# Pooled sums on TensorE in the first blocks, later x2 loads, and weights in rows of 2 KB

## The chip, the cores and the metric

The kernel runs on one core of a Trainium2 chip. Its engines are TensorE (PE in the profile; PEld is its weight load), VectorE (DVE), ScalarE (ACT), GpSimd (POOL) and SyncE (SP, which here only issues transfers). Each engine works through its own instructions in order, and semaphores tie the engines together. Transfers are issued on SP's and on ScalarE's queue and run on the same 16 DMA engines. The metric is the device time of one execution in microseconds, lower is better.

## The reference, cut to what matters

Three layers in fp32: an attention that is the sum of a pooled part (queries, keys and values averaged over 4 neighbouring tokens, the result repeated 4 times) and a local part (a band of 7 keys), then two feed-forward layers on all 2304 tokens.

```python
batch, n_heads, seq, head_dim = 4, 8, 576, 64; factor = 4
q_d = q.reshape(B, H, Sd, factor, D).mean(axis=3)      # k_d, v_d likewise
out_up = np.repeat(sm_attn(q_d, k_d, v_d), factor, axis=2)
mask = np.abs(pos[:, None] - pos[None, :]) < factor
scores = np.where(mask, scale * q @ k^T, -1e9)         # then softmax, @ v
x = out_up + out_local                                 # 2304 x 512
x = ((x @ w_a) * (x @ w_b)) @ w_out                    # d_ff 1536
h = x @ w_in; out = (h * clip(h + 3, 0, 6) / 6) @ w_out2   # d_ff 2048
```

## The kernel before

Large products run as three passes of a reduced fp32 format (fp32r): each operand is split into a first and a second part. Weights arrive as 64-bit numbers and are decoded on ScalarE and VectorE (`decode`): a tile of 1 MB, 128 partitions by 1024 numbers, is loaded into `raw`, one of two buffers, and passes through one step on ScalarE (`m`, L237), six on VectorE (L243 to L261), one more on ScalarE (L265) and one more on VectorE (L268), after which it is `wh`.

**The opening.** Attention is worked per batch b and group g of two heads. `pooled(b, g)` loads queries and keys side by side (`qk`; for the first batch the tile is called qk0, shown as qk) and values ordered by token within a neighbourhood of four (`vd` into `v` or `vraw`). It sums four tokens on VectorE (`sums`, L383; `add_v`, L378 and L379), multiplies (`score`, dsc, L392), takes the softmax (`top` on VectorE, `exps` on ScalarE, `inverse` and `norm` on VectorE), transposes on TensorE (`turn`, dpt), copies (`turned`, deT, ScalarE) and multiplies by the values (`pv`, dpo, L439); `keep` copies the result to `od`. `local(u)` does the same for a unit of 116 tokens (112 for the last of a batch, five units a batch) with scores sc (L479, L485), transposes pt (L516) and values po (L528); `total` adds the pooled part to po on VectorE (xf, L536), and `x_first` (ScalarE) and `x_second` (VectorE, L546) split the sum into the two parts of x.

**The first stage** (`job(n, f)`) multiplies the x of block n (2 or 3 units) by weight tile f, twice 12 matmuls (pab, L578), and stores the product of the two results, `a`, to `h_d`. **The second stage** (`second(n, f)`) loads `h` for a span of 512 tokens (256 in the last) on ScalarE's queue (L619), splits it on ScalarE (L623) and VectorE (L627), and multiplies (acc, L635); results go as `x2f` to `x2_d` (shown as x_d, L659). At the same time the weights w2o are decoded and stored again (`w_d`). **The third stage** (`inner`, `group`; ph, L747) loads x2 as `x2r` (L695) and **the fourth** (`outer`; oacc, L870) ends the kernel.

**Order.** All steps are handed to a planner (`Plan`) with an engine, an assumed duration, a due time (`want`), what they come after and which buffers they take. The planner plays the steps through with these assumed durations and writes each engine's instructions in the order in which they would begin. So a changed duration or due time moves instructions of all engines, also where the code is not touched. On the chip only that order, the semaphores and the buffers count.

Of the kernel before, what the change touches and what calls it, by code (L numbers as in the profile page):

```python
# [9 lines left out]
F32 = mybir.dt.float32  # L10
# [128 lines left out]
def fused_kernel(ctx: ExitStack, tc: tile.TileContext, qk, vt, vd, wab, wo, w2i, w2o, mask, out):  # L139
# [83 lines left out]
    def decode(src, want, put, tag, after=(), ahead=4, slack=1.0, raw=None, queue=None):  # L223
# [129 lines left out]
    def pooled(b, g, want):  # L353
# [21 lines left out]
        def add_v():  # L375
            v_ = T["v_"]
            T["v"] = v_[:, :, 0] if b == 0 else slot(ap, [HD, 2, P], F32, "dv", "dv")
            nc.vector.tensor_tensor(v_[:, :, 0:2], v_[:, :, 0:2], v_[:, :, 2:4], op=ALU.add)  # L378
            nc.vector.tensor_tensor(T["v"], v_[:, :, 0], v_[:, :, 1], op=ALU.add)  # L379

        def sums():
            T["s"] = slot(ap, [P, 2, SD], F32, "dqk", "dqk")
            nc.vector.tensor_reduce(T["s"], qks[b, g][:, :, HALO:HALO + S].rearrange("p a (s r) -> p a s r", r=FACTOR),  # L383
                                    axis=AX.X, op=ALU.add)

        def score():
            s = T["s"]
            sc = T["sc"] = two_banks("dsc")
            for a in range(2):
                for h in range(2):  # L390
                    r = slice(64 * h, 64 * h + 64)
                    nc.tensor.matmul(sc[:HD, h, a * SD:(a + 1) * SD], s[r, 0, a * HD:(a + 1) * HD], s[r, 1],  # L392
                                     start=True, stop=True)
# [40 lines left out]
        def pv():  # L434
            po = T["po"] = one_bank("dpo")
            for c in range(2):
                for h in range(2):
                    r = slice(64 * h, 64 * h + 64)
                    nc.tensor.matmul(po[r, :SD], T["v"][:, c, r], T["eT", c][:, h], start=(c == 0), stop=(c == 1))  # L439
# [9 lines left out]
        av = DVE(dve(768) + 0.06, want - 3, add_v, [lv], take=[] if b == 0 else ["dv"], give=[] if b == 0 else ["vraw"])  # L449
        i = DVE(dve(2 * S), want, sums, [ld], take=["dqk"])  # L450
        S_["sums", b, g] = i
        i = PE(0.5, want, score, [i], take=["s2"], give=["dqk"])
        i = DVE(dve(4 * SD) + 0.16, want, top, [i])
        i = ACT(4 * 0.47, want, exps, [i], take=["de"], give=["s2"])
        i = DVE(0.32, want, inverse, [i])
        i = DVE(dve(4 * SD), want, norm, [i])
        t = [PE(0.3, want, turn(c), [i], take=["b", "turn"], give=["de"] if c else []) for c in range(2)]
        t = [ACT(act(2 * SD), want, turned(c), [t[c]], take=["deT"], give=["b", "turn"]) for c in range(2)]
        i = PE(0.6, want, pv, [*t, av], take=["b", "pv"], give=["deT", "deT", "wh" if b == 0 else "dv"])
        S_["od", b, g] = ACT(act(SD), want, keep, [i, S_.get(("od", b, 0))], take=[] if g else ["od"], give=["b", "pv"])  # L460

    def local(u, want):
# [33 lines left out]
        def exps():  # L496
            e = L["e"] = slot(ap, [P, HP, 2, KB], F32, "e", "e")
            z = L["z"] = ap.tile([P, HP, 2], F32, tag="z", bufs=2, name="z")
            for p in range(HP):
                for h in range(2):  # L500
                    nc.scalar.activation(e[:, p, h], L["s4"][:, p, h], AF.Exp, bias=L["mx"][:, p, h:h + 1],  # L501
                                         scale=SCALE, accum_out=z[:, p, h:h + 1])
# [19 lines left out]
        def pv():  # L522
            po_ = one_bank("po")
            L["po"] = po_[:, :HP * UT].rearrange("d (p t) -> d p t", p=HP)
            for p in range(HP):
                for i in range(2):
                    for h in range(2):
                        nc.tensor.matmul(L["po"][64 * h:64 * h + 64, p, i * QB:(i + 1) * QB], v_[:, h, i, p],  # L528
                                         L["eT"][:, p, i * KB:i * KB + QB], start=True, stop=True)

        def total():
            xf = L["xf"] = slot(ap, [P, HP, UT], F32, "xf", "xf")
            n = tokens // FACTOR
            c = j * UT // FACTOR
            up = ods[b][:, :, c:c + n].unsqueeze(3).to_broadcast([P, HP, n, FACTOR])
# [618 lines left out]
```

## Time and profile before

| | |
|---|---|
| median of 3 runs | 973.01 us (971.87 to 974.76) |
| the profiled execution's own time | 975.95 us |
| its span in the trace | 974.2 us |
| TensorE busy | 927.7 us (95%) |
| VectorE busy | 766.0 us (79%) |
| ScalarE busy | 457.3 us (47%) |
| mean granted TensorE clock | 0.985 |

The span runs from the first to the last instruction; the execution's own time also holds what lies around it. A busy TensorE is not TensorE at its peak: the number of matmuls in a stretch and the granted clock say how fast it went.

### The profile page before, as it was taken

The page shows a single profiled execution, that of the slowest core. Times are in us where ns is not written, and L with a number is a line of the kernel's source. Part 1 is how long each engine was busy: PE and PEld are TensorE (multiplying, and loading weights), DVE is VectorE, ACT ScalarE, POOL GpSimd, SP SyncE. Part 2 cuts the span into 40 slices and gives each one's busy share as a digit, 9 for nine tenths or more (in the row PEclk, how much of TensorE's full clock was granted, in tenths as well). Part 3 has the DMA queues.
Part 4 walks back from the last instruction along what each step waited for, and adds up shares of the span by engine and source line. Part 5 has one row for each costly group of instructions (what it writes and reads, how often), then busy time and mean ns, then how long its engine had stood idle before and what let it go on. Part 6 is the DMA issues. An engine that isn't in the chain of part 4 may idle for free.

```text
span 974.2 us, 18526 instructions
## 1 busy us (share of the span) xinstructions
PE 927.7 (95%) x7040; PEld 869.7 (89%) x7040; DVE 766.0 (79%) x1390; ACT 457.3 (47%) x1164; POOL 5.2 (1%) x44
## 2 busy tenths in 40 slices
PE   3779999999999999999999898999999999999998
PEld 2568899999989999997877688999999999999998
DVE  6888898954746959686887644899898999997983
ACT  3765633445455424224444333545454665554551
POOL 1000000000000000000000000000000000000000
PEclk9988999999999999999999899999999999999999
DMA  8442755323314433325678664334327891815401
GB/s 259 173 122 82 243 163 192 127 84 99 112 49 132 169 136 133 131 95 204 214 241 271 219 211 147 104 142 164 122 108 256 274 295 43 265 39 167 159 17 49
DMA packets 90089, 151.21 MB, mean 155 GB/s; under 512 B 8208, under 2 KB 71696, under 8 KB 85648
## 3 DMA queue, kind: packets, MB, share of 16 engines
q1 hardware_dynamic: 80384, 132.54, 41.4%
q10 hardware_dynamic: 9616, 17.49, 5.7%
q8 instruction: 55, 0.90, 0.4%
q14 instruction: 34, 0.28, 0.1%
HBM read 100.19 MB, written 49.81 MB: 154 GB/s over the span
## 4 chain that ended last, share of the span: by engine, by line
PE 80%; DVE 9%; DMA 7%; ACT 2%; issue 2%; ACTq 0%; SPq 0%; DVEq 0%
PE pab L578 32%; PE ph L747 16%; PE oacc L870 15%; PE acc L635 9%; DMA h<-h_d 4%; PE po L528 2%; DVE in L678 2%; DMA vz<-vt 1%; PE sc L485 1%; PE pt L516 1%; PE dpo L439 1%; DVE e L843 1%; DVE w2o L1078 1%; PE dpt L424 1%; DMA raw<-wab 1%
## 5 line engine op out<-in xcount | busy, mean ns | idle before, releaser
L578 PE MATMUL pab<-x,wh 128*128 128x344 f32 (+2 forms) x2016 | 325.6, 320 | 1.9 <-DVE wh L268 1.7
L578 PEld LDWEIGHTS pab<-x,wh 128*128 128x128 f32 x2016 | 311.8, 192 | 4.7 <-DVE wh L268 2.0
L870 PE MATMUL oacc<-w2o,in 128*128 128x256 f32 x1512 | 182.1, 283 | 1.4 <-DVE in L678 1.4
L870 PEld LDWEIGHTS oacc<-w2o,in 128*128 128x128 f32 x1512 | 181.3, 191 | 2.2 <-DVE in L678 2.0
L747 PE MATMUL ph<-in,w 128*128 128x384 f32 x1008 | 177.3, 337 | 2.5 <-ACT in L675 2.3
L747 PEld LDWEIGHTS ph<-in,w 128*128 128x128 f32 x1008 | 176.7, 189 | 3.0 <-ACT in L675 2.5
L635 PE MATMUL acc<-h,wo 128*128 128x512 f32 (+1 forms) x720 | 156.5, 377 | 9.4 <-ACT h L623 8.3
L635 PEld LDWEIGHTS acc<-h,wo 128*128 128x128 f32 x720 | 126.7, 191 | 39.2 <-ACT h L623 10.8
L763 DVE TENSOR_TENSOR part<-ph,part 128x384 f32<-128x384 f32 x168 | 85.7, 549 | 9.6 <-PE ph L747 8.8
L584 ACT ACTIVATE a<-pab 128x344 f32<-128x344 f32 (+2 forms) x84 | 37.3, 447 | 95.8 <-PE pab L578 67.5
L771 ACT ACTIVATE r<-part,three 128x384 f32<-128x384 f32 x96 | 56.5, 613 | 52.9 <-DVE part L763 50.1
L587 DVE TENSOR_TENSOR a<-a,pab 128x344 f32<-128x344 f32 (+2 forms) x84 | 41.4, 493 | 50.3 <-PE pab L578 45.2
L627 DVE TENSOR_TENSOR h<-h 128x512 fp32r<-128x512 f32 (+1 forms) x60 | 37.4, 634 | 51.6 <-ACT h L623 51.3
L675 ACT ACTIVATE in<-gr 128x384 fp32r<-128x384 f32 x96 | 47.5, 521 | 41.0 <-PE oacc L870 31.2
L237 ACT ACTIVATE m<-raw 128x1024 f32<-128x1024 f32 x34 | 39.3, 1157 | 57.0 <-DVE raw L255 21.2
L623 ACT ACTIVATE h<-h 128x512 fp32r<-128x512 f32 (+1 forms) x60 | 34.9, 588 | 64.5 <-DMA h<-h_d 51.6
L678 DVE TENSOR_TENSOR in<-gr,in 128x384 fp32r<-128x384 f32 x96 | 49.5, 551 | 6.7 <-ACT in L675 6.2
L675 ACT ACTIVATE in<-e 128x384 fp32r<-128x384 f32 x72 | 36.5, 527 | 33.9 <-PE oacc L870 20.2
L774 DVE SCALAR_TENSOR_TENSOR r<-r,part 128x384 f32<-128x384 f32 x96 | 50.4, 548 | 1.2 <-ACT r L771 1.1
L501 ACT ACTIVATE e<-sc,mx 128x64 f32<-128x64 f32 x160 | 47.6, 328 | 5.5 <-DVE mx L494 4.4
L255 DVE SCALAR_TENSOR_TENSOR raw<-raw,m 128x1024 f32<-128x1024 uint32 x34 | 41.7, 1227 | 1.2
L261 DVE TENSOR_TENSOR raw<-raw 128x1024 f32<-128x1024 f32 x34 | 41.5, 1221 | 0.5
(82 smaller groups left out, 885.7 us busy)
## 6 DMA issues: line engine op xcount, KB each, us to landing
g_d<-r SPq DMA_DIRECT2D x96, 192.0 KB
gr<-g_d SPq DMA_DIRECT2D x48, 384.0 KB
h<-h_d ACTq DMA_DIRECT2D x48, 256.0 KB
raw<-wab SPq DMA_DIRECT2D x10, 1024.0 KB
h_d<-a SPq DMA_DIRECT2D x48, 172.0 KB
raw<-w2i SPq DMA_DIRECT2D x8, 1024.0 KB
raw<-w2o SPq DMA_DIRECT2D x8, 1024.0 KB
qk<-qk SPq DMA_DIRECT2D x14, 576.0 KB
```

The lines of the kernel that those rows point to most:

```text
L255: nc.vector.scalar_tensor_tensor(out=lo.bitcast(F32), in0=lo, scalar=2.0 ** -52, in1=m, op0=ALU.mult, op1=ALU.mult)
L261: nc.vector.tensor_tensor(v, v, lo.bitcast(F32), op=ALU.add)
L501: nc.scalar.activation(e[:, p, h], L["s4"][:, p, h], AF.Exp, bias=L["mx"][:, p, h:h + 1], scale=SCALE, accum_out=z[:, p, h:h + 1])
L578: nc.tensor.matmul(T[k], wab_t[f][:, x, c], xs[n][:, g, y, :nb], start=(g == 0 and i == 0), stop=(g == KC - 1 and i == 2))
L635: nc.tensor.matmul(accs[n][e], wo_t[f // 2][:, x, c], hs[n, f][:, y], start=(f == 0 and i == 0), stop=(f == F1 - 1 and i == 2))
L675: nc.scalar.activation(x[0][:, 0], src(), AF.Copy)
L678: nc.vector.tensor_tensor(x[0][:, 1], src(), x[0][:, 0], op=ALU.subtract)
L747: nc.tensor.matmul(acc[k], t[:, x, g * P:(g + 1) * P], X[k, g][0][:, y], start=(g == 0 and n == 0), stop=(g == 1 and n == 2))
L763: nc.vector.tensor_tensor(s[name], acc[k], s[other], op=ALU.add)
L771: nc.scalar.activation(T["r"], src(), AF.Relu, bias=three)
L774: nc.vector.scalar_tensor_tensor(out=T["r"], in0=T["r"], scalar=6.0, in1=src(), op0=ALU.min, op1=ALU.mult)
L870: nc.tensor.matmul(acc[n][e], X[n, k][0][:, x, e * P:(e + 1) * P], t[:, y], start=(k == 0 and i == 0), stop=(k == K - 1 and i == 2))
```

## The change

It has five parts. (1) In the first batch (`soon`), VectorE sums only the keys; the scores take the queries of the four tokens apart, as four matmuls into one accumulation, and the value product takes the four values apart in the same way. (2) In the units of the first three blocks that have all 116 tokens (seven units), TensorE adds the pooled part: a matmul of the identity with `od`, each column repeated four times, opens the accumulation of po, and x is split from po itself. (3) The four x2 loads of the first pair in the third stage come after the step `second(last span, 1)`. (4) A weight tile lies in memory as four blocks of 128 rows of 2 KB, no longer as 128 rows of 8 KB. (5) The first two weight tiles are loaded on SP's queue, no longer on ScalarE's; `exps` of a unit is four steps instead of one, and some due times and assumed durations change.

```diff
         def load():
             T["raw"] = slot(xp if raw == "x" else dp, [P, W], mybir.dt.uint64, raw or "raw", "raw")
-            (queue or nc.sync).dma_start(T["raw"], src)
+            (queue or nc.sync).dma_start(T["raw"].rearrange("p (a c) -> p a c", a=CUT), src.rearrange("a p c -> p a c"))
...
-    def pooled(b, g, want):
+    def pooled(b, g, want, soon):
...
+            a = slice(1, 2) if soon else slice(0, 2)
             T["s"] = slot(ap, [P, 2, SD], F32, "dqk", "dqk")
-            nc.vector.tensor_reduce(T["s"], qks[b, g][:, :, HALO:HALO + S].rearrange("p a (s r) -> p a s r", r=FACTOR),
-                                    axis=AX.X, op=ALU.add)
+            nc.vector.tensor_reduce(T["s"][:, a], tokens()[:, a], axis=AX.X, op=ALU.add)
...
+                part = slice(a * HD, (a + 1) * HD)
+                for i in range(FACTOR if soon else 1):
+                    for h in range(2):
+                        r = slice(64 * h, 64 * h + 64)
+                        nc.tensor.matmul(sc[:HD, h, a * SD:(a + 1) * SD], tokens()[r, 0, part, i] if soon else s[r, 0, part],
+                                         s[r, 1], start=(i == 0), stop=(not soon or i == FACTOR - 1))
...
+            v = [T["v_"][:, :, i] for i in range(FACTOR)] if soon else [T["v"]]
             for c in range(2):
-                for h in range(2):
-                    r = slice(64 * h, 64 * h + 64)
-                    nc.tensor.matmul(po[r, :SD], T["v"][:, c, r], T["eT", c][:, h], start=(c == 0), stop=(c == 1))
+                for i, x in enumerate(v):
+                    for h in range(2):
+                        r = slice(64 * h, 64 * h + 64)
+                        nc.tensor.matmul(po[r, :SD], x[:, c, r], T["eT", c][:, h], start=(c == 0 and i == 0),
+                                         stop=(c == 1 and i == len(v) - 1))
...
-        av = DVE(dve(768) + 0.06, want - 3, add_v, [lv], take=[] if b == 0 else ["dv"], give=[] if b == 0 else ["vraw"])
+        av = lv if soon else DVE(dve(768) + 0.06, want - 1, add_v, [lv], take=["dv"], give=["vraw"])
...
+            if soon:
+                nc.tensor.matmul(L["po"].rearrange("p a (s r) -> p a s r", r=FACTOR), ident, pooled_part(), start=True, stop=False)
...
+            if soon:
+                L["xf"] = L["po"]
...
-        i = ACT(8 * 0.42, want, exps, [i], take=["e"], give=["s2"])
+        for p in range(HP):
+            i = ACT(2 * 0.31, want, exps(p), [i], take=[] if p else ["e"], give=["s2"] if p == HP - 1 else [])
...
-            return DMA(NB, want - 12 if p else want - 6, run, S_["x2d", m[t]] + ([] if p == 0 else [opened]),
+            return DMA(NB, want - 12 if p else want - 6, run,
+                       S_["x2d", m[t]] + [S_["second", len(spans) - 1, 1] if p == 0 else opened],
                        take=["x0" if p == 0 else "L"])
...
-        local(u, t)
+        local(u, t, m < 3 and unit_tokens(u) == UT)
...
-                                queue=nc.scalar if f < 2 else None)
+                                queue=None)
...
+        w = w.reshape(-1, P, CUT, w.shape[2] // CUT).transpose(0, 2, 1, 3)
         res[name] = np.ascontiguousarray(w).view(np.uint64)
```

What the planner makes of it is seen best at three places. A row's line is that of its own kernel, so line numbers differ between the two.

TensorE, the program's first rows, before: the four groups' scores stand together, then transposes, the values of the first group, and the first local scores.

```order
L392 MATMUL dsc<-dqk 72x144 x16
L424 MATMUL dpt<-ident,de 72x72 x8
L439 MATMUL dpo<-deT,v_146 64x144 x4
L424 MATMUL dpt<-ident,de 72x72 x4
L479 LDWEIGHTS ident_88
L479 MATMUL sc<-mask_sb,ident_88 128x256
```

The same place in the changed kernel:

```order
L398 MATMUL dsc<-dqk,qk_113 72x144 x16
L398 MATMUL dsc<-dqk,qk_117 72x144 x16
L398 MATMUL dsc<-dqk,qk_121 72x144 x16
L430 MATMUL dpt<-ident,de 72x72 x4
L490 LDWEIGHTS ident_88
L490 MATMUL sc<-mask_sb,ident_88 128x256
```

One group's scores are now 16 matmuls, and three groups stand ahead of the first transposes; the fourth group's scores come after the first local scores and the first group's values.

SP, the program's first rows, before (v are the values of the first batch, vz those of the local units, the qk row with x4 is the second batch):

```order
L365 DMA qk_113<-qk 128x2x576
L365 DMA qk_121<-qk 128x2x576
L370 DMA v_146<-vd 72x1024
L370 DMA v_156<-vd 72x1024
L370 DMA v_161<-vd 72x1024
L370 DMA v_178<-vd 72x1024
L473 DMA vz_105<-vt 64x512 x2
L473 DMA vz_106<-vt 64x512 x2
L365 DMA qk<-qk 128x2x576 x4
```

The same place in the changed kernel, from the last value load on:

```order
L370 DMA v_215<-vd 72x1024
L229 DMA raw<-wab 128x4x256 x2
L484 DMA vz_105<-vt 64x512 x2
L484 DMA vz_106<-vt 64x512 x2
L365 DMA qk<-qk 128x2x576 x4
```

The first two weight tiles, which before stood on ScalarE behind the exponentials and around the first two copies deT, now stand behind the values and ahead of the local values.

SP near the end of the second stage, before: three x2 loads behind a weight tile, with stores of decoded weights after them.

```order
L229 DMA raw<-w2o 128x1024
L695 DMA x2r<-x_d_5448 128x2x384 x2
L695 DMA x2r<-x_d_5446 128x2x384
L1040 DMA w_d_112<-ws 128x4x256
L1040 DMA w_d_112<-ws 128x3x256
```

In the changed kernel, further on: the four x2 loads stand after the stores of span 3 (the last with 512 tokens) and ahead of those of span 4.

```order
L683 DMA x_d_6245<-x2f 128x384
L683 DMA x_d_6247<-x2f 128x128
L719 DMA x2r<-x_d_5527 128x2x384
L719 DMA x2r<-x_d_5529 128x2x384 x2
L719 DMA x2r<-x_d_5527 128x2x384
```

The x2 loads have moved from behind a weight tile in the middle of the stage to its last span; the other transfers on SP there keep their order but for one pair of stores and for steps that pass each other.

## Rows read from the trace of the kernel before

**Rows 1.** The page: the span, and busy time of each engine.

```profile
span 974.2 us, 18526 instructions
...
PE 927.7 (95%) x7040; PEld 869.7 (89%) x7040; DVE 766.0 (79%) x1390; ACT 457.3 (47%) x1164; POOL 5.2 (1%) x44
```

**Rows 2.** Stretches: length, busy us (instructions) by engine, granted clock, DMA, GB/s.

```profile
0.00:55.00 55.00, 30.47 (x376) 21.68 (x376) 42.71 (x80) 29.52 (x126) 3.97 (x28) 0.97 0.69 213
55.00:115.00 60.00, 54.96 (x643) 48.95 (x640) 52.12 (x95) 37.58 (x160) 0.64 (x8) 0.89 0.40 126
441.60:607.50 165.90, 156.46 (x722) 126.55 (x720) 110.21 (x173) 65.00 (x113) 0.00 (x0) 0.98 0.67 218
```

**Rows 3.** Waits from 0 to 55 us: total, times, longest.

```profile
ACT m L237 <- DMA raw<-wab: 3.6, 1, 3.6
```

**Rows 4.** Timeline of TensorE in the opening: start, length, what, idle before.

```profile
6.73 1.24 PE L392 MATMUL dsc<-dqk 64*72 64x144 f32 x8 [6.73 <-DVE dqk L383]
...
19.80 1.23 PE L439 MATMUL dpo<-deT,v 72*64 72x144 f32 x8 [0.55 <-ACT deT L431]
...
43.51 1.96 PE L528 MATMUL po<-eT,vz 128*64 128x58 f32 x32 [0.69 <-ACT eT L520]
...
47.94 1.16 PE L528 MATMUL po<-eT,vz 128*64 128x58 f32 x32
...
55.01 2.91 PE L578 MATMUL pab<-x,wh 128*128 128x232 f32 x12
...
62.36 0.71 PE L392 MATMUL dsc<-dqk 64*72 64x144 f32 x8
```

**Rows 5.** Timeline of VectorE in the opening.

```profile
11.21 1.35 DVE L383 TENSOR_REDUCE dqk<-qk 128x288 f32<-128x1152 f32 x1 [2.18 <-DMA qk<-qk]
...
28.06 0.69 DVE L243 TENSOR_SCALAR m<-m 128x1024 f32<-128x1024 f32 x1 [2.55 <-ACT m L237]
...
53.74 0.59 DVE L546 TENSOR_TENSOR x<-xf,x 128x464 fp32r<-128x464 f32 x1
```

**Rows 6.** VectorE's groups from 0 to 55 us: count, busy us, mean ns.

```profile
L383 DVE TENSOR_REDUCE dqk<-qk 128x288 f32<-128x1152 f32 x5 | 6.8, 1352 | 6.9 <-DMA qk<-qk 6.6
...
L397 DVE TENSOR_REDUCE dmx<-dsc 72x4 f32<-72x576 f32 x4 | 3.0, 739 | 0.0
L345 DVE TENSOR_TENSOR e<-e,z 128x512 f32<-128x512 f32 x4 | 2.7, 682 | 0.0
L378 DVE TENSOR_TENSOR v<-v 72x512 f32<-72x512 f32 x4 | 2.7, 680 | 0.0
...
L379 DVE TENSOR_TENSOR v<-v 72x256 f32<-72x256 f32 x4 | 1.7, 421 | 0.1
...
L536 DVE TENSOR_TENSOR xf<-po,od 128x464 f32<-128x464 f32 x2 | 1.3, 636 | 0.3 <-PE po L528 0.3
```

**Rows 7.** Stretches again, columns as in rows 2.

```profile
20.00:25.00 5.00, 3.83 (x50) 2.57 (x48) 4.11 (x12) 2.07 (x11) 0.00 (x0) 1.00 1.06 410
535.00:550.00 15.00, 10.62 (x33) 7.62 (x32) 6.97 (x10) 3.22 (x5) 0.00 (x0) 0.77 0.71 242
560.00:575.00 15.00, 15.00 (x67) 12.31 (x66) 6.08 (x11) 3.90 (x7) 0.00 (x0) 1.00 0.88 288
595.00:600.00 5.00, 3.60 (x27) 3.06 (x26) 1.60 (x4) 1.57 (x4) 0.00 (x0) 1.00 0.80 263
```

**Rows 8.** The chain that ended last, near 534 us: start, length, what.

```profile
534.13 8.48 DMA h<-h_d
```

**Rows 9.** Timeline of TensorE from 530 to 548 us.

```profile
543.31 4.93 PE L635 MATMUL acc<-h,wo 128*128 128x512 f32 x10 [4.38 <-ACT h L623]
```

**Rows 10.** Timeline of SP's issues in the second stage.

```profile
533.67 0.78 SPq L229 DMA_DIRECT2D raw<-w2o  x1
534.50 3.00 SPq L695 DMA_DIRECT2D x2r<-x_d  x3
...
593.72 16.03 SPq L659 DMA_DIRECT2D x_d<-x2f  x8
```

More of the change, by code (lines that the diff above doesn't have):

```diff
@@ L448, in pooled, with local @@
         lv = DMA(290, early + 1 + 0.1 * g, load_v, take=["wh" if b == 0 else "vraw"])
-        av = DVE(dve(768) + 0.06, want - 3, add_v, [lv], take=[] if b == 0 else ["dv"], give=[] if b == 0 else ["vraw"])
-        i = DVE(dve(2 * S), want, sums, [ld], take=["dqk"])
+        av = lv if soon else DVE(dve(768) + 0.06, want - 1, add_v, [lv], take=["dv"], give=["vraw"])
+        i = DVE(dve(S if soon else 2 * S), want, sums, [ld], take=["dqk"])
         S_["sums", b, g] = i
-        i = PE(0.5, want, score, [i], take=["s2"], give=["dqk"])
+        i = PE(2.0 if soon else 0.5, want, score, [i], take=["s2"], give=["dqk"])
         i = DVE(dve(4 * SD) + 0.16, want, top, [i])
-        i = ACT(4 * 0.47, want, exps, [i], take=["de"], give=["s2"])
+        i = ACT(4 * 0.37, want, exps, [i], take=["de"], give=["s2"])
         i = DVE(0.32, want, inverse, [i])
         i = DVE(dve(4 * SD), want, norm, [i])
[L457 to L462, printed above, removed]
+        t = [PE(0.3, want, turn(c), [i], take=["b", "turn", "deT"], give=["de"] if c else []) for c in range(2)]
+        t = [ACT(act(2 * SD), want, turned(c), [t[c]], give=["b", "turn"]) for c in range(2)]
+        i = PE(1.6 if soon else 0.6, want, pv, [*t, av], take=["b", "pv"] + ([] if g else ["od"]),
+               give=["deT", "deT", "wh" if b == 0 else "vraw" if soon else "dv"])
+        S_["od", b, g] = ACT(act(SD), want, keep, [i, S_.get(("od", b, 0))], give=["b", "pv"])
+    def local(u, want, soon):
         L = {}
@@ L494, in top, with exps, run @@
             nc.vector.tensor_scalar(mx, mx, SCALE, None, op0=ALU.mult)
[L496 to L499, printed above, removed]
+        def exps(p):
+            def run():
+                if p == 0:
+                    L["e"] = slot(ap, [P, HP, 2, KB], F32, "e", "e")
+                    L["z"] = ap.tile([P, HP, 2], F32, tag="z", bufs=2, name="z")
                 for h in range(2):
-                    nc.scalar.activation(e[:, p, h], L["s4"][:, p, h], AF.Exp, bias=L["mx"][:, p, h:h + 1],
-                                         scale=SCALE, accum_out=z[:, p, h:h + 1])
+                    nc.scalar.activation(L["e"][:, p, h], L["s4"][:, p, h], AF.Exp, bias=L["mx"][:, p, h:h + 1],
+                                         scale=SCALE, accum_out=L["z"][:, p, h:h + 1])
+            return run
         def inverse():
@@ L548, in local @@
         n = HP * UT
-        ld = DMA(128, want - 25 if u < 2 else want - 5, load, [S_.get(("pv", u - 2))])
+        ld = DMA(128, want - 20 if u < 2 else want - 5, load, [S_.get(("pv", u - 2))])
         last = j == NU - 1
@@ L641, in second @@
         i = DVE(dve(nb), want - 12, h_second, [i])
-        i = PE(12 * (0.009 + 0.00044 * nb), want, products, [i, S_["wo", f // 2], S_["ps"]],
+        i = S_["second", n, f] = PE(12 * (0.009 + 0.00044 * nb), want, products, [i, S_["wo", f // 2], S_["ps"]],
                take=["q"] * KC if f == 0 else [],
@@ L940, in fused_kernel @@
             for g in range(HP):
-                pooled(u // NU, g, t - 0.05 + 0.01 * g)
-        local(u, t)
+                pooled(u // NU, g, t - 0.05 + 0.01 * g, u // NU < 1)
+        local(u, t, m < 3 and unit_tokens(u) == UT)
     for f in range(F1):
```

35 lines of the change are left out of this document (19 added, 16 removed).

## The prediction

> **What bounds the kernel now.** I read the page first, then stretches, then who waits for whom, then the rows of the stretches that lose time. TensorE is busy 927.7 of 974.2 us [rows 1], so only about 46 us can come from waits, and work added to TensorE where it never waits costs its full length. Three stretches hold nearly all of the loss [rows 2]. From 0 to 55 us TensorE is busy for 30.5 of 55 us. From 55 to 115 it is busy for 55.0 of 60, but at a granted clock of 0.89. From 441.6 to 607.5 (the second stage) it is busy for 156.5 of 165.9. VectorE is busy 42.7 of the first 55 us and 52.1 of the next 60, so in the opening it is nearly the bound. Of its waits one has to do with a transfer that the change moves: ScalarE stands 3.6 us before the first weight tile [rows 3].
>
> The opening ends where TensorE issues its first product of the first stage, at 55.01 [rows 4]. In front of it VectorE runs almost without a gap from 28.06, where it stops waiting for that weight tile, to 54.3, where the second unit's x is finished [rows 5].
>
> **What VectorE loses.** Half of each of four sums of queries and keys: 4 x 1.35 / 2 = 2.7 us; the value sums: 4 x (0.68 + 0.42) = 4.4 us; the addition of the pooled part in seven units: 7 x 0.63 = 4.4 us [rows 6]. Together 11.5 us, 8.4 of it before 55 us.
>
> **What TensorE gains.** A group's scores are 4 matmuls (8 rows of the profile, as each fp32 matmul shows two) and become 16; likewise its value products. Eight rows take 1.24 and 1.23 us early in the opening, but 0.71 at 62.36 [rows 4]. The clock column shows 1.00 for both, so for the early rows I go by their length, which is that of half speed. A group then pays 3.7 us more for scores and 3.7 for values at half speed, 2.1 and 2.1 at full. The pooled part by identity (128 x 464, fp32) has no row. Bounds from the score rows at full speed: 0.71 / 4 = 0.18 us for one of two matmuls of 144 columns that share the array, so 464 / 144 x 0.18 = 0.57 if a full-height one costs as much, 1.14 if it costs as much as the pair. I take 0.9, since nothing shares the array with it. So the opening's TensorE work grows by 17 us at full speed for the four groups and by 2.7 for three units.
>
> **Does TensorE reach full speed in time?** The product po took 1.96 us at 43.51 and 1.16 at 47.94, after 4.4 us almost without a pause [rows 4]. In the new order scores 0 and 1 stand behind each other as 64 rows, so I expect the change about 5 us after TensorE's start.
>
> **The new chain of the opening.** Score 0 starts at 6.73 - 0.7 = 6.0 (half a sum less) and takes 4 x 1.24 = 5.0 at half speed, to 11.0. Score 1 takes 2.7 (a little at half speed), to 13.7. Score 2 has its load by 11.2 [rows 5] and ends at 16.5. A transpose, a local score and a transpose take about 1.4, the values of group 0 take 2.8, and score 3, behind them, ends near 23.5. From there VectorE has all its work. What it does up to the second unit's x is what it did from 28.06 to 54.3 (26.3 us), without two additions of the pooled part (1.3) and one value sum (1.1, now later), with a full sum (1.35), the last group's maximum (0.74) and one rescaling (0.68) more [rows 6]: 26.7 us, which ends at 50.2. The weights no longer hold it: their two loads stand behind the values and not behind ScalarE's transposes, and should land near 20 instead of 26.9. The first product then begins near 51 instead of 55.0: **4 us**. TensorE has by then done one more po, one more transpose and one score (2.3 us at full speed) that it owed later; it still owes four identity products (3.6). VectorE is spared four more additions (2.5) in a stretch where it is 87% busy; I count 2. Opening: 4 + 2.3 - 3.6 + 2 = **4.7 us**. The order adds one wait: the first identity product stands on TensorE until ScalarE has copied the last group's pooled part, with the local scores of unit 4 and all else behind it; in the chain above that is at about 40, while VectorE has work until 50, so I count nothing (bound 1.5). The bank of po is held until the second part of x is done, one VectorE step (0.6) longer, of four banks: nothing. Scores read their weights at a step of four tokens, which no row shows: nothing, at worst the added 17 us twice, which is rival 1. The first local values now load behind the weights, near 22, and are needed near 40. Bounds of the opening: if the clock rises only after score 1, score 3 ends 2 to 5 us later and nothing is left; if all that VectorE loses came through, 11.
>
> **The second stage.** The worst place is 535 to 550: 33 matmuls where 560 to 575 has 67 [rows 7], at 0.224 us each, so 7.5 us lost, part idle and part at the lower clock (0.77). The chain shows a load of h of 8.48 us from 534.13, and TensorE's row at 543.31 that it had stood for 4.38 us [rows 8, 9]. Just ahead SP issued a weight tile of 1 MB (533.67) and, from 534.50, three of the four x2 loads of the third stage, 1.18 MB [rows 10]. The change takes these three away. At the 242 and 288 GB/s of these two windows they are 4.9 or 4.1 us of DMA time. So h that comes 4.1 us sooner leaves 0.3 of the 4.38, too short, I think, for the clock to fall. I count **6.5 us**.
>
> The x2 loads now stand on SP behind the first four of the eight stores at 593.72 [rows 10], so near 595.5. They are 1.57 MB: 6.0 us at 263 GB/s, over near 602, and the stage ends at 607.5, so the third stage does not wait for them. But they fall beside the last loads of h: 595 to 600 already has 27 matmuls of 128x256 where 44 fit at half of 0.224 us [rows 7]. I take 1.5 us of loss (bounds 0 and 3).
>
> Rows of 2 KB for the weights: a window in which weight tiles moved in 8 KB rows (20 to 25 us) shows 410 GB/s at a share of 1.06, one with shorter rows (595 to 600) 263 at 0.80, that is 387 against 329 at a full share [rows 7]. A tile of 1.05 MB then takes 3.2 us instead of 2.7, 0.5 longer. In the opening this is hidden by the 7 us that the weights are early; in the first stage by VectorE, which has a tile ahead; in the second, ScalarE stands in order before a weight tile, with h behind it, so up to 8 x 0.5 = 4 us could show. Against that h, on ScalarE's queue, meets shorter rows on SP's. Bounds: 4 us lost, 4 gained (the other short waits of this stage); I take 0.5 gained. SP needs more time to issue 512 rows than 128, but stands in no chain.
>
> The Trainium skill, DMA: Bandwidth & Descriptors (Specifications), states that 512 B is enough for line rate; by it the 0.5 us per tile would not exist and the loss bound of 4 us would be nothing. The two windows speak against it, but they differ in more than the rows; no run here shows weights in 2 KB rows.
>
> **Sum.** 4.7 + 6.5 - 1.5 + 0.5 = 10.2 us. The profiled execution took 975.95 us (span 974.2), which gives 965.8; it stands 2.9 above the median of the three runs (973.01), so I forecast 963.
>
> **Rivals.**
> 1. Slower: TensorE stays at half speed through the opening and becomes its bound. Added work: 4 x 7.4 + 3 x 1.8 = 35 us; with the 30.5 there now, from 6.0 on, the first product starts at 71.5, 16.5 later. Less 5.5 from the second stage: 984. It decides once the added work exceeds the 18.5 us in which TensorE is idle between 6 and 55 and what full speed takes off the old work. For it: every row up to 43 us is at half-speed length. Against it: 64 rows without a gap. Chance 0.11.
> 2. Only the second stage gains: TensorE's additions eat what VectorE gives: 967.5. Chance 0.18.
> 3. Only the opening gains: h is late for other reasons (ScalarE's order, weights that land later): 968.3. Chance 0.14.
> 4. The change does nothing that can be measured, as VectorE's savings turn into waits for TensorE and the x2 loads cost at 595 what they cost at 535: 973. Chance 0.10.
> 5. More: the shorter rows also let h pass the weights in the other short waits. The second stage is idle for 165.9 - 156.5 = 9.4 us [rows 2], 4.4 of it in the wait at 543; of the other 5.0 I give 3 to this: 960. For it: the load of h at 534 landed only when what was queued ahead of it on the other queue had passed. Against it: some of these waits end with ScalarE's order and not with a load. Chance 0.14. The Trainium skill, DMA: Bandwidth & Descriptors (Queues, rings and completion order), states that a DMA engine takes turns between its queues packet by packet; by it this case is the outcome, and no run here shows it.
> 6. The forecast, both gains: 963, itself from 957 to 967. Chance 0.33.
>
> **How the numbers follow.** A measurement of this kernel tells 0.3% (2.9 us) from no change. Cases 5, 6, 2 and 3 lie below 970, case 4 within 2.9 of 973, case 1 above; a few hundredths of 2 and 3 fall short of 970: faster 0.75, same 0.13, slower 0.12. The range leaves out case 1, the upper part of case 4, and gains beyond 18 us: 955 to 973.
>
> **What would show it.** Right: the first product near 51 us; the eight rows of scores as 32 rows, the later groups in about 2.8 us; no wait of ScalarE for the first weight tile; VectorE without a gap from about 23; 535 to 550 at full count and clock; the x2 loads at about 595, landing before 607. Wrong: early scores of 5 us each through 25 us; waits for DMA of h that move to 595 to 602; longer waits of ScalarE for weights in the second stage.

## The result and the profile after

The changed kernel takes 963.55 us (median of 4, 962.18 to 964.19); the kernel before took 972.44 beside it (970.22 to 974.76). The ratio is 0.9892, 95% interval 0.9866 to 0.9917, so it is faster by 0.8 to 1.3%. The forecast of 963 holds. Its terms don't, so the number is luck: the opening gave more than twice what was counted, and the second stage gave nothing.

The profiled execution took 964.17 us. Its page, as in [rows 1]:

```profile
span 962.2 us, 18896 instructions
...
PE 932.5 (97%) x7246; PEld 875.6 (91%) x7246; DVE 755.3 (78%) x1375; ACT 455.8 (47%) x1164; POOL 5.6 (1%) x44
```

TensorE does 206 more instructions and VectorE is busy 10.7 us less. Where the span's 12.0 us went is read from the first row of each stage on TensorE's timeline:

| first row of | before | after | gained in the stretch up to it |
|---|---|---|---|
| pab, the first product of the first stage | 55.01 | 51.12 | 3.9 |
| acc, the second stage | 441.62 | 430.21 | 7.5 |
| ph, the third stage | 609.87 | 599.52 | -1.1 |
| end of the span | 974.2 | 962.2 | 1.7 |

So 11.4 us were there before the second stage began. Three stretches of the changed kernel, columns as in [rows 2]:

```profile
0.00:51.00 51.00, 40.89 (x584) 33.15 (x584) 37.37 (x71) 31.14 (x134) 3.96 (x28) 0.90 0.80 234
51.00:111.00 60.00, 59.61 (x730) 52.26 (x725) 56.71 (x101) 37.95 (x141) 1.03 (x8) 1.00 0.43 131
430.20:599.50 169.30, 156.55 (x722) 127.40 (x720) 110.34 (x173) 65.59 (x116) 0.00 (x0) 0.98 0.68 216
```

The 60 us after the first product are the surprise: before, TensorE waited 5.0 us of them and its granted clock was 0.89; now it waits 0.4 at 1.00. At 0.89, 55 busy us hold 48.9 us of full-speed work, so about 6.0 us went to the clock. VectorE is busy 56.7 of the 60 us, where it was 52.1. The second stage is about as long as it was.

(For the opening the clock column reads too high; see the last section.) TensorE's timeline in the opening, to be held against [rows 4]:

```profile
6.07 9.25 PE L398 MATMUL dsc<-dqk,qk 64*72 64x144 f32 x96 [6.07 <-DVE dqk L388]
...
16.97 2.18 PE L448 MATMUL dpo<-deT,v 72*64 72x144 f32 x32
19.08 2.42 PE L398 MATMUL dsc<-dqk,qk 64*72 64x144 f32 x32
...
39.79 1.92 PE L539 MATMUL po<-od,ident 128*128 128x464 f32 x2 [0.39 <-ACT od L454]
...
45.14 1.30 PE L539 MATMUL po<-od,ident 128*128 128x464 f32 x2
...
49.17 0.94 PE L539 MATMUL po<-od,ident 128*128 128x464 f32 x2
...
51.12 2.94 PE L602 MATMUL pab<-x,wh 128*128 128x232 f32 x24
```

And VectorE's, against [rows 5]: decoding begins at 24.25 without a wait, and the second unit's x is finished at 49.0.

```profile
24.25 0.69 DVE L243 TENSOR_SCALAR m<-m 128x1024 f32<-128x1024 f32 x1
...
48.40 0.63 DVE L567 TENSOR_TENSOR x<-po,x 128x464 fp32r<-128x464 f32 x1
```

In the second stage the wait of [rows 9] has become two. TensorE's timeline, and below it the chain that ended last at the same places:

```profile
534.72 0.50 PE L659 MATMUL acc<-h,wo 128*128 128x512 f32 x1 [2.66 <-ACT h L647]
...
591.06 6.40 PE L659 MATMUL acc<-h,wo 128*128 128x256 f32 x36 [2.54 <-ACT h L647]
```

```profile
527.95 6.06 DMA h<-h_d
...
584.40 6.18 DMA h<-h_d
```

SP's issues, as in [rows 10], show what moves beside these two loads: the weight tile is still there in front of the first, and the x2 loads now stand in front of the second.

```profile
527.11 0.54 SPq L229 DMA_DIRECT2D raw<-w2o  x1
...
582.13 2.38 SPq L719 DMA_DIRECT2D x2r<-x_d  x4
```

### The profile page after: what moved, and what is told of

The parts are those of the page before. It is cut to its first block, busy times and chain, and to the rows that moved or that the text cites. A ratio compares the mean times of both kernels' runs of the same rounds, so it can differ in the third digit from the quotient of the medians.

```text
span 962.2 us, 18896 instructions
## 1 busy us (share of the span) xinstructions
PE 932.5 (97%) x7246; PEld 875.6 (91%) x7246; DVE 755.3 (78%) x1375; ACT 455.8 (47%) x1164; POOL 5.6 (1%) x44
## 4 chain that ended last, share of the span: by engine, by line
PE 84%; DVE 8%; DMA 6%; issue 1%; ACT 1%; ACTq 0%; SPq 0%; DVEq 0%
PE pab L602 32%; PE ph L772 18%; PE oacc L895 15%; PE acc L659 10%; DMA h<-h_d 4%; PE po L543 2%; PE dsc L398 2%; DVE in L702 2%; PE sc L496 1%; PE pt L529 1%; PE dpo L448 1%; DMA raw<-w2o 1%; DVE e L868 1%; PE po L539 1%; PE dpt L430 1%
## 5 line engine op out<-in xcount | busy, mean ns | idle before, releaser
L602 PE MATMUL pab<-x,wh 128*128 128x344 f32 (+2 forms) x2016 | 319.8, 317 | 0.1
L602 PEld LDWEIGHTS pab<-x,wh 128*128 128x128 f32 x2016 | 306.4, 188 | 3.6 <-issue 1.8
L659 PE MATMUL acc<-h,wo 128*128 128x512 f32 (+1 forms) x720 | 156.5, 378 | 10.7 <-ACT h L647 9.6
L651 DVE TENSOR_TENSOR h<-h 128x512 fp32r<-128x512 f32 (+1 forms) x60 | 37.5, 636 | 49.1 <-ACT h L647 48.9
L248 DVE SCALAR_TENSOR_TENSOR raw<-raw,m 128x1024 uint32<-128x1024 uint32 x34 | 41.5, 1221 | 0.2
```

Source lines behind the costliest of these rows:

```text
L248: nc.vector.scalar_tensor_tensor(out=hi, in0=hi, scalar=0xC0000000, in1=T["m"].bitcast(U32), op0=ALU.bitwise_and, op1=ALU.bitwise_or)
L602: nc.tensor.matmul(T[k], wab_t[f][:, x, c], xs[n][:, g, y, :nb], start=(g == 0 and i == 0), stop=(g == KC - 1 and i == 2))
L659: nc.tensor.matmul(accs[n][e], wo_t[f // 2][:, x, c], hs[n, f][:, y], start=(f == 0 and i == 0), stop=(f == F1 - 1 and i == 2))
```

## The experiments

The theory after this reading: the gain comes from the opening alone, and there from VectorE. Rivals: the second stage's edits are worth what was predicted and something else hides it; TensorE's fuller work holds the clock up; the earlier weights did it. Ratios are to the kernel before, timed beside it, and medians are over several executions; what is read from a trace is one execution. A change of code or of buffers also lets the planner order the steps anew; where that matters it is said.

### The second stage's two edits

**x2 loads released as before** (`x2_as_before`):

```diff
-                       S_["x2d", m[t]] + [S_["second", len(spans) - 1, 1] if p == 0 else opened],
+                       S_["x2d", m[t]] + ([] if p == 0 else [opened]),
```

> The changed kernel with the four x2 loads of the third stage released as before (no wait for the last span's second step). Theory (the opening gives nearly all, the move of the x2 loads trades the stall at 534 us for one at 591 us): within 1.5 us of the changed kernel, 962 to 965; the wait of acc for h near 591 us (2.5 us in the changed kernel) is gone, and one near 525 to 535 us grows to about 4.4 us. Rival (the move saves what the prediction counted, 6.5 less 1.5): 968 to 969.

961.22 us (957.04 to 968.06), ratio 0.9885 (0.9851 to 0.9919): no loss, against the rival. The six times lie up to 11 us apart, and the profiled execution is the fastest. In it the waits of acc for ScalarE's part of h in the second stage sum to 3.8 us, the longest 1.1, though three x2 loads (522.55) stand again right behind the weight tile, so the wait of 4.4 us that the theory expected did not come:

```profile
PE acc L659 <- ACT h L647: 3.8, 5, 1.1
```

**Weights in rows of 8 KB** (`rows_8k`):

```diff
-            (queue or nc.sync).dma_start(T["raw"].rearrange("p (a c) -> p a c", a=CUT), src.rearrange("a p c -> p a c"))
+            (queue or nc.sync).dma_start(T["raw"], src)
...
-        w = w.reshape(-1, P, CUT, w.shape[2] // CUT).transpose(0, 2, 1, 3)
```

> The changed kernel with a weight tile as 128 rows of 8 KB again. Theory (the rows' length is worth next to nothing): within 1.5 us of the changed kernel, 962 to 965. Rival A (short rows let h pass the weights): 966 to 968, with longer waits of acc for h in the second stage. Rival B (short rows cost, as the changed kernel's second stage is 1 us longer in the trace): 960 to 962.

963.43 us (961.82 to 965.99), ratio 0.9891 (0.9866 to 0.9916), which is that of the changed kernel. The second stage has much the same waits in both: here one of 1.94 us at 532 and one of 2.94 at 589.

**Both undone** (`opening_only`: the two diffs above together).

> The changed kernel with both undone: x2 loads released as before, weights in rows of 8 KB. What is left is TensorE's additions, the queue of the first two weights and the steps of the exponentials. Theory: 961 to 965, with the second stage starting near 430 us and lasting 168 to 169 us. Rival (the second stage's edits are worth the 5.5 us of the prediction): 968 to 970.

962.52 us (962.22 to 964.49), ratio 0.9884 (0.9861 to 0.9907). The second stage begins at 430.89 and lasts 167.3 us. Everything is there without the two edits. With the x2 loads back beside the long load of h, the wait there is 2.80 us, where the changed kernel has 2.66 without them:

```profile
531.65 0.50 PE L659 MATMUL acc<-h,wo 128*128 128x512 f32 x1 [2.80 <-ACT h L647]
```

**These two alone, on the kernel before** (`second_stage_only`).

> The kernel before with two of the edits alone: x2 loads after the last span's second step, weights in rows of 2 KB. Theory: no difference from before that can be measured, 970.5 to 974, second stage starting near 441 us. Rival (the prediction's sum for the second stage, 5.5 us): 966 to 968.

977.43 us, ratio 1.0028 (1.0009 to 1.0046): if anything slower. TensorE's timeline shows why the move brings nothing: the wait of 4.38 us [rows 9] is 3.09 without the x2 loads beside it, and two waits stand near where these now are (SP issues them at 593.09), where the kernel before has one of 1.32.

```profile
542.96 0.50 PE L635 MATMUL acc<-h,wo 128*128 128x512 f32 x1 [3.09 <-ACT h L623]
...
593.11 6.33 PE L635 MATMUL acc<-h,wo 128*128 128x256 f32 x48 [2.07 <-ACT h L623]
...
601.10 6.37 PE L635 MATMUL acc<-h,wo 128*128 128x256 f32 x36 [1.67 <-ACT h L623]
```

The kernel before, at its end of the stage:

```profile
598.35 9.18 PE L635 MATMUL acc<-h,wo 128*128 128x256 f32 x72 [1.32 <-ACT h L623]
```

There 72 matmuls take 9.18 us; here the last 36 take 6.37, at a granted clock of 0.76 from 600 to 607 us (1.00 there in the kernel before). The same count made for all six kernels, over the 720 matmuls of acc, shows what the move of the x2 loads is worth in each of its two places (us between the starts of two matmuls, one execution each):

| x2 loads and rows | from the 361st to the 421st | from the 661st to the last |
|---|---|---|
| early, 8 KB: before | 21.6 | 7.0 |
| late, 2 KB: `second_stage_only` | 19.2 | 10.8 |
| early, 8 KB: `opening_only` | 19.8 | 7.0 |
| late, 8 KB: `rows_8k` | 17.0 | 12.1 |
| early, 2 KB: `x2_as_before` | 15.9 | 7.0 |
| late, 2 KB: changed kernel | 17.3 | 11.7 |

In all three pairs the late loads cost 3.8 to 5.1 us at the end of the stage; in the middle they give 2.4 and 2.8 us in two pairs and lose 1.4 in the third, whose early side is the fastest execution of its kernel.

In the opening this kernel differs from the one before in the length of the rows alone, and there it is not free. Issued on ScalarE's queue at the same time (18.81 and 18.95), the first weight tile holds ScalarE up for 7.7 us, where it was 3.6 [rows 3], and the first product comes at 58.37, where it was 55.01:

```profile
ACT m L237 <- DMA raw<-wab: 7.7, 1, 7.7
```

### The opening: VectorE's relief or TensorE's work

**VectorE sums again** (`vector_sums`): all else as changed.

```diff
-                pooled(u // NU, g, t - 0.05 + 0.01 * g, u // NU < 1)
-        local(u, t, m < 3 and unit_tokens(u) == UT)
+                pooled(u // NU, g, t - 0.05 + 0.01 * g, False)
+        local(u, t, False)
```

The due time and buffers of `add_v` for the first batch are those of before.

> The changed kernel with all of TensorE's additions undone: VectorE sums queries and values and adds the pooled part, as before; queue of the first weights, steps of the exponentials, x2 loads and 2 KB rows as in the changed kernel. Theory A (the gain comes from VectorE's 11.5 us alone) and theory B (it comes from TensorE being kept at work, so that its clock does not fall in the 60 us after the first product): both 971 to 976, first product near 55 us, granted clock of the next 60 us about 0.9. Rival (the earlier weights and the finer steps give it): 963 to 966.

974.93 us, ratio 1.0015 (0.9992 to 1.0039): the whole gain is gone. The weights were early here too (VectorE's decoding begins at 24.59), and the first product comes at 52.19, not near 55 as expected. But in the 60 us after it TensorE waits 4.5 us at a granted clock of 0.91 (the profiled execution, 982.02 us, is the slowest of the ten):

```profile
52.20:112.00 59.80, 55.31 (x648) 49.63 (x646) 55.13 (x102) 37.96 (x157) 0.64 (x8) 0.91 0.47 148
```

**The same with TensorE's work added to no use** (`vector_sums_and_pe_work`): each pooled score four times, pooled values four times over, the identity product ahead of po, all overwritten.

```diff
-                for i in range(FACTOR if soon else 1):
+                for i in range(FACTOR if b == 0 else 1):
...
+            for c in [0] * (6 if b == 0 else 0):
+                for h in range(2):
+                    r = slice(64 * h, 64 * h + 64)
+                    nc.tensor.matmul(po[r, :SD], T["v"][:, c, r], T["eT", c][:, h], start=True, stop=True)
```

> The kernel of the run above with TensorE's work of the changed kernel added to it without use: each pooled score four times over, the pooled values four times over, the identity product ahead of po, all overwritten by the result as before. VectorE is relieved of nothing. Theory A (VectorE's relief): no gain, 973 to 980. Theory B (the clock): granted clock at 0.97 or more in the 60 us after the first product, and 965 to 970, though TensorE has 15 to 20 us more to do.

987.62 us, ratio 1.016 (1.0122 to 1.0197). The work costs 12.7 us and does not hold the clock: 0.87 and 0.81 in 60 to 80 and 80 to 100 us. Theory B falls.

```profile
60.00:80.00 20.00, 18.24 (x202) 15.82 (x201) 17.08 (x35) 9.58 (x41) 0.00 (x0) 0.87 0.37 114
80.00:100.00 20.00, 17.12 (x218) 12.75 (x218) 17.25 (x32) 13.86 (x66) 0.00 (x0) 0.81 0.10 34
```

**VectorE relieved, TensorE not loaded** (`no_pe_work`): one query and one value of four are used and the pooled part is left out in seven units, so its output lacks these.

```diff
-                for i in range(FACTOR if soon else 1):
+                for i in range(1):
...
-            v = [T["v_"][:, :, i] for i in range(FACTOR)] if soon else [T["v"]]
+            v = [T["v_"][:, :, 0]] if soon else [T["v"]]
...
-            if soon:
-                nc.tensor.matmul(L["po"].rearrange("p a (s r) -> p a s r", r=FACTOR), ident, pooled_part(), start=True, stop=False)
```

> The changed kernel without what TensorE takes over: the pooled scores of the first batch use one query of four, its pooled values one value of four, and the seven units leave out the pooled part (so the output lacks these). VectorE is relieved as in the changed kernel. Theory A: at least as fast as the changed kernel, 955 to 963. Theory B: the first product comes earlier, but the clock falls again in the 60 us behind it (0.95 or less), 964 to 970.

960.23 us, ratio 0.9884 (0.9851 to 0.9916). Theory A holds. Behind the first product TensorE has its full clock here too (columns as in [rows 2]), so theory B's loss does not come:

```profile
0.00:49.50 49.50, 33.93 (x387) 24.34 (x387) 37.84 (x72) 31.35 (x138) 3.96 (x28) 1.00 0.84 245
49.50:110.00 60.50, 58.36 (x723) 52.75 (x722) 56.99 (x101) 37.38 (x138) 0.95 (x8) 1.00 0.43 133
```

Its second stage begins at 428.27, 1.9 us before the changed kernel's: that is what TensorE's 206 rows cost in the end. Most of them go into time in which TensorE waited: in the opening it stands still for 15.6 us here and for 10.1 in the changed kernel.

**The pooled part on VectorE again** (`vector_pooled_part`): `local(u, t, False)`, the sums stay on TensorE.

> The changed kernel with the pooled part added by VectorE again in the seven units (no identity product); queries and values still summed on TensorE. Theory A: VectorE has 4.4 of its 11.5 us again, 966 to 969. Theory B: TensorE loses 7 us of its 24 us of added work, most of it at full clock behind the first product, 963 to 966.

968.86 us, ratio 0.9958 (0.9934 to 0.9982), 5 us above the changed kernel for seven additions of 0.63 us on VectorE, 4.4 in all. Theory A's number. The trace shows where they count: the first product comes 2.7 us earlier (48.47), with no identity product on TensorE ahead of it, but from there to acc it takes 383.9 us instead of 379.1.

### The opening: the queue of the first weights

**The first two weights on ScalarE's queue again** (`weights_on_act`); the orders of TensorE and VectorE are those of the changed kernel.

```diff
-                                queue=None)
+                                queue=nc.scalar if f < 2 else None)
```

> The changed kernel with the first two weight tiles loaded on ScalarE's queue again. Theory A (VectorE is the bound of the opening, so each wait of VectorE there counts): ScalarE again stands some 3 us before the first tile, VectorE's decoding begins near 27 us instead of 24.3, and the time is 965 to 967. Rival (the tile is early enough on either queue, VectorE has other work): 962 to 965.

974.43 us, ratio 1.0011 (0.9987 to 1.0036). Both theories missed it: this edit alone also loses the whole gain (the profiled execution, 971.23 us, is the second fastest of the ten). ScalarE's timeline shows two waits, and VectorE's and TensorE's what they do (three views, one after the other):

```profile
20.12 0.41 ACT L437 ACTIVATE deT<-dpt 72x288 f32<-72x288 f32 x1 [3.77 <-DMA vz<-vt]
...
31.14 1.12 ACT L237 ACTIVATE m<-raw 128x1024 f32<-128x1024 f32 x1 [4.30 <-DMA raw<-wab]
```

```profile
32.29 0.69 DVE L243 TENSOR_SCALAR m<-m 128x1024 f32<-128x1024 f32 x1 [3.50 <-ACT m L237]
```

```profile
59.52 2.95 PE L602 MATMUL pab<-x,wh 128*128 128x232 f32 x24
```

The copy deT at 20.12 needs no transfer. It stands behind the issue of the weight tile (19.68), which by the trace waits until a load of local values on the other queue has landed (why for that load, no run here shows); so ScalarE stands for 3.8 us with a group's softmax behind it, and for 4.3 more until the tile is there. The first product comes at 59.52 and acc at 438.63, both 8.4 us later than in the changed kernel. The Trainium skill, DMA: Bandwidth & Descriptors (Issuing engines are not separate DMA queues), states that transfers run on the same 16 DMA engines whoever starts them, and that another issuing engine only saves the time to initiate. Here the queue was worth 8.4 us, by when the tile is issued (19.68 here, 5.25 on SP's queue) and by what stands behind the issue on its engine. Part of it belongs to the rows of 2 KB: with them the tile lands 11.4 us after its issue here, while in the kernel before ScalarE goes on with it 8.0 us after its issue (18.95 to 26.91).

The four kernels with rows of 2 KB and late x2 loads side by side (ratios to before):

| | weights on ScalarE's queue | on SP's queue |
|---|---|---|
| VectorE adds | 1.0028 | 1.0015 |
| TensorE adds | 1.0011 | 0.9892 |

Neither edit alone gives anything clear of the intervals; together they give 1.4%. Where each one counts is read from the traces (us, one execution each):

| | first product | from there to acc |
|---|---|---|
| before | 55.01 | 386.6 |
| `second_stage_only`: VectorE adds, ScalarE's queue | 58.37 | 382.0 |
| `vector_sums`: VectorE adds, SP's queue | 52.19 | 390.6 |
| `weights_on_act`: TensorE adds, ScalarE's queue | 59.52 | 379.1 |
| changed kernel: TensorE adds, SP's queue | 51.12 | 379.1 |

The queue decides when the first product comes, the additions how long the stretch behind it takes. While VectorE still adds, a first product that comes 6.2 us earlier is paid back behind it (8.6 us, in an execution that is the slowest of its kernel); with VectorE relieved, the stretch behind is as short with either queue, and the late tile costs its 8.4 us in the opening alone.

The upper left kernel of the square also lacks the steps of the exponentials and the other due times and durations, and the change moves more than its list says: TensorE's steps, no longer ScalarE's, take the buffers deT, eT and od. What these are worth by themselves was not run.

### What holds the second stage

**Five buffers for h** (`h_five_buffers`), paid for with two of three buffers for the copies of acc:

```diff
-            "hg1": 1, "xo": 3, "q": 8, "ws": 2, "x0": 4, "L": 24, "c": 14}
+            "hg1": 2, "xo": 1, "q": 8, "ws": 2, "x0": 4, "L": 24, "c": 14}
...
-        return slot(pools["p3" if f % 4 == 3 else "p2"], [P, 2, NC], F32R, f"hg{f % 4 // 3}", name)
+        return slot(pools["p3" if f % 5 >= 3 else "p2"], [P, 2, NC], F32R, f"hg{int(f % 5 >= 3)}", name)
```

> The changed kernel with five buffers for h instead of four, paid for by one buffer for the copies of acc instead of three. A step of the second stage is 12 matmuls of 0.224 us, 2.7 us, so four buffers hide a load, its split and its wait for a turn only up to about 8 us. Theory C (the waits near 534 and 591 us are loads of h that take longer than four buffers hide, whatever is beside them): the waits of acc for h fall from 9.6 us to under 5, 958 to 961. Rival D (the transfers as such are the limit there, or the single copy buffer gives the waits back): 963 to 968.

958.53 us (955.75 to 960.53), ratio 0.984 (0.9798 to 0.9882): faster than the kernel before, and its slowest execution lies below the changed kernel's fastest, though the two intervals touch. TensorE's waits in the second stage (us in total, times, longest), first those of the changed kernel:

```profile
PE acc L659 <- ACT h L647: 9.6, 6, 2.7
PE ph L772 <- ACT in L699: 2.1, 1, 2.1
```

And with five buffers:

```profile
PE ph L772 <- ACT in L699: 6.5, 1, 6.5
PE acc L659 <- ACT h L647: 0.7, 1, 0.7
```

The 9.6 us in six waits of the changed kernel are 0.7, and the stage lasts 159.3 us instead of 169.3. About 4.5 us of it go back at its end, where ph waits 6.5 us instead of 2.1: with one buffer left, each copy of acc waits for the store before it, as ScalarE's timeline shows.

```profile
584.29 0.38 ACT L676 ACTIVATE x2f<-acc 128x256 f32<-128x256 f32 x1 [1.81 <-DMA x_d<-x2f]
586.49 0.38 ACT L676 ACTIVATE x2f<-acc 128x256 f32<-128x256 f32 x1 [1.82 <-DMA x_d<-x2f]
```

**The same with the x2 loads as before** (`h_five_buffers_x2_as_before`).

> The same five buffers, with the x2 loads released as before. Theory C: the three x2 loads in the middle of the stage are hidden too, 956 to 960. Rival D: 961 to 967.

957.94 us (956.33 to 959.24), ratio 0.9835 (0.9795 to 0.9875): the same. Acc waits 1.8 us for ScalarE's part of h, so the three loads in the middle are hidden. The planner orders the steps anew with the buffers; that is not separated from the fifth buffer itself.

**The loads of h on GpSimd's queue** (`h_on_pool_queue`):

```diff
-            nc.scalar.dma_start(h[:, 1].bitcast(F32), h_d[f][:, lo:hi])
+            nc.gpsimd.dma_start(h[:, 1].bitcast(F32), h_d[f][:, lo:hi])
```

> The changed kernel with the loads of h on GpSimd's queue, so that they stand behind no work of ScalarE. Theory E (the wait near 534 us comes from h loads that ScalarE issues late, as it stands in order before a weight tile): the wait there goes to about 1 us, the waits of acc for h halve, 958 to 961. Rival (h is late because of what moves beside it or for want of buffers): 962 to 966, waits as in the changed kernel.

966.25 us (963.26 to 967.5), ratio 0.9914 (0.9885 to 0.9943). Theory E falls: acc still waits 5.9 us for ScalarE's part of h and 4.5 for VectorE's (9.6 and 0.9 in the changed kernel).

## Why the prediction was right, and where it was not

**The total** is right by luck, from two errors of about the same size and opposite sign: the opening gave 11.4 us instead of 4.7, the second stage lost 1.1 instead of giving 5.5. The remaining 1.7 fell behind it, where no term stood, and no run shows what gave it. Rival 3 (only the opening gains) was what happened, with an opening worth more than its 4.7.

**The chain of the opening held.** Score 0 began at 6.07 (6.0 forecast), TensorE came to full speed near 11, the forecast's 5 us after its start (21 rows in the 2 us before 11, 56 in the 4 us behind), the three scores ended at 15.3 (16.5), score 3 at 21.5 (23.5), the second unit's x at 49.0 (50.2), the first product at 51.12 (51). The identity product takes 0.94 us at full speed (0.9), the wait before the first one 0.39 (counted as nothing, bound 1.5). The tile is there when ScalarE comes to it at 22.27, and the 3.6 us of [rows 3] are gone. That VectorE's relief gave these 4 us is less sure: it waits 5.2 us for the longer scores, which it did not before, and `vector_sums`, in an order of its own, has its first product only 1.1 us later with all additions on VectorE.

**The step that failed in the opening** is "VectorE is spared four more additions (2.5) in a stretch where it is 87% busy; I count 2". It took the 60 us behind the first product as fixed but for these additions. In them TensorE stood still for 5.0 us and ran at a lower clock. Of these waits 1.7 us end with weights that VectorE has just decoded, and the longest (2.0 us at 70.40, for ScalarE's exponentials) lies on a chain that runs through VectorE's steps from 64.2 on. A VectorE that enters the stretch ahead removes nearly all of it. Up to the second stage TensorE waits 3.3 us less and no longer loses the 6.0 us of clock; against that it has 2.3 us more to do there: four identity products (3.8) and a local score (1.1), less a po, a transpose and a pooled score that it had done before (2.5). That is 7.0 of the 7.5 us found. The prediction's upper bound (11 us, if all that VectorE loses comes through) is about what was measured: VectorE is busy 323.5 us before the second stage where it was 334.4. `vector_sums`, `no_pe_work` and `vector_pooled_part` show from three sides that it is VectorE's relief and not TensorE's fuller work. It needs the early weights as well: `weights_on_act` has a VectorE just as little busy (323.8) and comes to acc only 3.0 us before the kernel before.

**The weights' queue was given too little.** In "the weights no longer hold it" it is a cover for 7 us of slack; `weights_on_act` shows that without it the opening loses 8.4 us and the kernel its whole gain. I had charged only the wait for the tile and not the wait of ScalarE at the issue itself, with a softmax behind it. TensorE's additions with rows of 8 KB on ScalarE's queue were not run; `vector_sums` differs from the changed kernel in the planner's order too, so the table above is not a clean square.

**The step that failed in the second stage** is "h that comes 4.1 us sooner leaves 0.3 of the 4.38": it charged the whole long load to the three x2 loads beside it. Without them the wait is 3.1 us in the kernel before and 2.7 in the changed kernel; with them in the new opening it is 2.8 in `opening_only` and at most 1.1 in the profiled execution of `x2_as_before`. The 6.5 us counted for this place were 2.4 and 2.8 in two pairs of the table above and nothing in the third. The other term, 1.5 us of loss at the end (bound 3), was 3.8 to 5.1: the late loads bring waits of 2 to 3 us there and a lower clock behind them (0.89 from 585 to 600 us in the changed kernel). What decides is how long four buffers can hide a load. A step is 2.7 us of matmuls; four buffers hide a load of the usual 4 us, but not one of 6 to 8.5, whatever it meets on the way. The fifth buffer removes nearly all of these waits with every transfer in place.

**Rows of 2 KB** were counted at +0.5 with bounds of 4 us on either side. With the weights on SP's queue `rows_8k` puts them at nothing that can be measured. Rival 5's rule of the Trainium skill (DMA: Bandwidth & Descriptors, Queues, rings and completion order), by which shorter rows would let h pass, shows in no time: 963.55 us with rows of 2 KB, 963.43 with rows of 8 KB. That page of the Trainium skill also has 512 B for line rate (Specifications), and for the weights on SP's queue the runs agree: rows of 2 KB cost nothing there. In the opening, on ScalarE's queue beside the loads of SP, they did cost: 3.4 us of the first product (`second_stage_only`). The two windows from which I took 387 against 329 GB/s differed in more than their rows, as the prediction itself said.

**Rival 1** (TensorE at half speed through the opening) did not come: 96 score rows took 9.25 us, the later group's 32 rows 2.42. It shows in part where TensorE has to wait: with the weights on ScalarE's queue the granted clock of the first 50 us is 0.86, and group 3's 32 score rows take 3.93 us.

## What to carry to other kernels

Where one engine feeds another, look past the first place at which the chain meets: time taken off the feeder comes back in every later stretch in which the fed engine waits or has lost its clock, until the feeder is no longer behind. Starting the fed engine earlier is worth nothing while the feeder is behind. A long transfer next to a wait is not yet its cause; ask how long the buffers hide a transfer, since a load moved out of the way of one wait lands beside the next. An issue on the queue of an engine that computes is an instruction in that engine's order, and it can wait there for a transfer that the program never names.

## What the runs showed of the hardware that was not expected

In the changed kernel the clock falls once more within the opening. From 20 to 35 us TensorE is busy 12.1 of 15 us, with waits of up to 1.2 us; from about 35 to 45 its granted clock is half, 1.2 of 2.4 GHz (columns as in [rows 2]):

```profile
20.00:35.00 15.00, 12.13 (x226) 10.08 (x224) 13.30 (x24) 11.81 (x46) 0.00 (x0) 1.00 0.85 247
...
35.00:40.00 5.00, 3.82 (x33) 2.90 (x31) 4.89 (x9) 3.33 (x21) 0.00 (x0) 0.54 0.65 211
40.00:45.00 5.00, 5.00 (x68) 3.14 (x68) 4.31 (x8) 3.25 (x14) 0.00 (x0) 0.50 0.25 66
45.00:50.00 5.00, 5.00 (x60) 3.09 (x55) 4.71 (x12) 3.85 (x16) 0.00 (x0) 0.93 0.78 263
```

In 40 to 45 TensorE is busy without a gap and still at half; the identity product takes 1.92 us at 39.79, 1.30 at 45.14 and 0.94 at 49.17.

The column tells nothing of the time before TensorE first comes to full speed: it reads 1.00 there, so its mean over an opening is too high (0.97 in [rows 2], 0.90 in the changed kernel). In `no_pe_work` it reads 1.00 over the whole opening, while TensorE's timeline has half-speed lengths up to 49 us and full ones only behind the first product:

```profile
18.12 1.25 PE L398 MATMUL dsc<-dqk,qk 64*72 64x144 f32 x8 [0.69 <-ACT de L412]
...
47.59 1.97 PE L541 MATMUL po<-eT,vz 128*64 128x58 f32 x32
...
52.73 0.71 PE L398 MATMUL dsc<-dqk 64*72 64x144 f32 x8
```

So TensorE's additions do lift the clock within the opening (rows of full length from about 11 to 35 us in the changed kernel), and it earns nothing there: the kernel that runs its opening at half speed has its first product at 49.49, earlier than 51.12.
